# Half of w_down loaded early, and the last head's wo product summed in four column groups of one PSUM bank

## The chip, the cores and the metric

The kernel runs on one core of a Trainium2 chip. The metric is the device time of one execution in microseconds (us), the median of several runs. The profile measures the same execution from its first to its last instruction (the "span"); a run's time is about 1.8 us above its span (1285.2 against 1283.4 us for the profiled run of the kernel before).

Names used below: PE is TensorE, PEld its weight loads, DVE VectorE, ACT ScalarE, SP the engine that issues the DMAs. FFN2 is the product with w_down, PV the product with the values, oT its transposed and scaled result, FIN the product of oT with the last head's rows of wo. "Cold" means at the halved clock, "warm" at the full one.

## The reference, cut to what matters

One token is decoded. Attention has 8 key/value heads of 65536 positions and 16 query heads; a small FFN runs on the same normalized row, and everything is summed into one row of 448.

```python
# cut: shapes of the parts that matter
D = 448; Hq, Hkv, Sk, Dh = 16, 8, 65536, 256; F = 1792
xn = layernorm(x)                                # [1, 448]
o = softmax(q @ k.T * Dh**-0.5) @ v              # k, v caches: 2 x 268 MB in bf16
A = o.reshape(1, Hq * Dh) @ wo                   # wo [4096, 448]
g, u = silu(xn @ w_gate), xn @ w_up              # [1, 1792]
y = ((g * u) @ w_down) * sigmoid(xn @ w_r)       # w_down [1792, 448]
out = x + A + xn + y
```

The caches must be read once from HBM. All weights together are about 12 MB.

## The kernel before: the parts that the change touches

The caches go through a ring of four 4 MB slots. A "unit" is a quarter of a head; there are U = 4 units in each of 8 heads. While the keys of one head are worked on, the values of the head before it are. The last head's values are loaded alone, at the end, the very last slot in four pieces of 2, 1, 0.5 and 0.5 MB, so that little work is left when the last bytes land. The DMA program, issued in this order by SP:

```python
    item("wq", ...)
    for u in range(U):                       # keys of head 0
        ...
        if u == U // 2 - 1:
            item("wg", [... w_gate and w_up into w_area ...], [("QT",)])
            item("wd_a", [(wd_a[:, :], wd_src(0), "wd")])       # first half of w_down, 0.8 MB
    for t in range(NT): ...                  # keys of head h+1 and values of head h
    for t in range(NT, NU): ...              # values of the last head
    item("wd_b", [(w_area[:, 0:WDN], wd_src(1), "we0")], [("FFN1",)])   # second half, over w_gate
    for i in range(rep):                     # the last head's rows of wo, 2 x 0.23 MB
        item(("wo_end", i), [...])
    W("sp", "RESULT")
    ... out[0] <- res_bf[:, :]               # one row of 448
```

Between the last keys and the last values PE does the FFN as far as it can (`middle`); after the last values it does the rest (`ending`):

```python
    def middle():
        ...
        pe_ffn1(); pe_tot(NT); pe_ffn_hT()
        pe_ffn2(0, "wd_a", wd_a)             # 7 matmuls [128 x 1]^T @ [128 x 448]

    def ending():
        T = NU - 1
        dve_ob(T)                            # evict o from PSUM
        pe_oT(T)                             # transpose, and scale by 1/sum on DVE: oT
        pe_ffn2(1, "wd_b", w_area)           # 7 more
        ...
        O("dve", "BASE", ... base_f = ps_y * sigmoid + base_f ...)
        for i in range(rep):
            W_item("pe", ("wo_end", i))
            O("pe", ("FIN", i), lambda it, i=i: attn_mm(ps_fin, wo_end[:, :], [i], i == 0, i == rep - 1))  # 2 matmuls of 448
        O("dve", "RESULT", lambda it: nc.vector.tensor_tensor(out=res_bf[:, :], in0=ps_fin, in1=base_f, op=ALU.add))
```

PV, the product with the values, already uses four column groups of the PE array: four matmuls with four weight columns each run side by side and write to PSUM partitions 0, 32, 64 and 96.

## Time and profile before

| | before |
|---|---|
| time, median of 3 runs | 1284.51 us (1284.49 to 1285.25) |
| time and span of the profiled run | 1285.2 us, 1283.4 us |
| moved | 549 MB, 428 GB/s over the span |
| PE / DVE / ACT busy | 72% / 46% / 36% |
| from the start of the last PV to the end | 8.3 us |

First the page: the span in 40 slices, with the clock granted to PE in tenths (9 is full), the share of busy DMA engines and what they moved.

```profile
PEclk9988888998889988879888889888899887898876
DMA  9999999999999999999999999999999999999997
GB/s 405 427 433 427 433 432 431 430 431 432 432 433 431 433 430 433 430 433 430 433 432 432 432 431 432 429 433 433 431 432 432 432 430 433 431 431 433 431 429 318
```

DMA is full in every slice but the last, whatever PE's clock does. The view of waits, for the queue on SP that issues the DMAs, says what it waits for (us in total, times, longest):

```profile
SPq L776 <- PE ps_t L352: 855.3, 58, 20.9
SPq L776 <- PE ps_o L352: 182.8, 60, 18.6
SPq L776 <- PE ps_m L352: 145.9, 7, 22.7
```

These are waits for ring slots to come free, while the stream of earlier issues keeps the engines busy. So bytes set the time up to the last value, and what follows the last value is added to it. That tail, from the timeline (start, us, engine, line, operation, count, [idle before <- who ended it]):

```profile
1275.08 0.60 PE L352 MATMUL ps_o<-ring,p_sb 128*4 128x512 bf16 x4 [0.67 <-DMA ring<-in_A_v_cache_dram]
...
1276.79 0.16 DVE L561 TENSOR_TENSOR oT_sb<-ps_m,rs 128x4 bf16<-128x4 f32 x1 [0.36 <-PE ps_m L352]
...
1276.94 2.77 PE L352 MATMUL ps_t<-w_area,hT_sb 128*1 128x448 bf16 x7 [0.20 <-DMA w_area<-in_B_w_down_dram]
...
1279.51 1.70 PE L352 MATMUL ps_s<-wo_end,oT_sb 128*1 128x448 bf16 x4
...
1281.25 0.61 DVE L727 TENSOR_TENSOR res_bf<-ps_s,rowsf 1x448 bf16<-1x448 f32 x1 [0.82 <-PE ps_s L352]
1281.89 0.32 SPq L776 DMA_DIRECT2D out_dram<-res_bf  x1
```

The last PV begins at 1275.08 us, when its values have landed. oT is ready at 1276.95. The second half of w_down lands at about the same time: the wait of 0.20 us before the first matmul of `ps_t` is put down to it. Then come seven matmuls of w_down (`ps_t`) and four of wo (`ps_s`), 0.37 us from one to the next, then an add of 0.61 us over 448 columns in one partition, then the output. The windows view has the clock (columns: window and its us, then busy us and count of PE, PEld, DVE, ACT and POOL, the granted clock, DMA share, GB/s):

```profile
1274.00:1276.00 2.00, 1.01 (x8) 0.09 (x4) 0.27 (x1) 0.00 (x0) 0.00 (x0) 0.50 0.78 311
1276.00:1278.00 2.00, 1.32 (x7) 0.52 (x8) 0.59 (x2) 0.00 (x0) 0.00 (x0) 0.50 0.19 70
1278.00:1280.00 2.00, 2.00 (x7) 0.74 (x6) 0.24 (x1) 0.00 (x0) 0.00 (x0) 0.50 0.00 0
```

The clock in this stretch is half of the full one.

### The profile page before, as it was taken

Reading aid. Unit: us, or ns where it says so; the run is one execution under the profiler, and the core shown is the slowest. Engines: PE = TensorE matmul, PEld = TensorE weight load, DVE = VectorE, ACT = ScalarE, POOL = GpSimd, SP = SyncE. Lnnn points to the kernel's source line nnn. Section 1 sums busy time; section 2 is a strip of 40 time slices with the busy share of each in tenths; the row PEclk is TensorE's granted clock in tenths of the full one; section 3 lists DMA queues with packets and bytes.
Section 4 is the critical chain, followed back from the end, with each engine's and each line's share of the span. In section 5 each row is a group of like instructions: output and inputs, shape, how many; then the busy total and the mean of one; then the engine's idle time right before and its main releaser. Section 6 shows DMA issues by size and latency. Waiting matters only on the chain.

```text
span 1283.4 us, 22878 instructions
## 1 busy us (share of the span) xinstructions
PE 924.9 (72%) x9824; PEld 671.5 (52%) x9824; DVE 585.8 (46%) x1091; ACT 459.2 (36%) x655; POOL 4.5 (0%) x35
## 2 busy tenths in 40 slices
PE   3988766786666886666876667866668766678654
PEld 3867554465454565554654545654446544456411
DVE  4756443554344554444554445543445534455300
ACT  2645332353333443324433243432434333234300
POOL 1000000000000000000000000000000000000000
PEclk9988888998889988879888889888899887898876
DMA  9999999999999999999999999999999999999997
GB/s 405 427 433 427 433 432 431 430 431 432 432 433 431 433 430 433 430 433 430 433 432 432 432 431 432 429 433 433 431 432 432 432 430 433 431 431 433 431 429 318
DMA packets 22228, 549.22 MB, mean 428 GB/s; under 512 B 2371, under 2 KB 4422, under 8 KB 5190
## 3 DMA queue, kind: packets, MB, share of 16 engines
q1 hardware_dynamic: 22210, 549.04, 99.6%
q8 instruction: 8, 0.13, 0.0%
q14 instruction: 6, 0.05, 0.0%
q10 hardware_dynamic: 4, 0.00, 0.0%
HBM read 549.03 MB, written 0.00 MB: 428 GB/s over the span
## 4 chain that ended last, share of the span: by engine, by line
DMA 68%; PE 31%; SPq 0%; ACT 0%; issue 0%; DVE 0%
DMA ring<-in_A_k_cache_dram 63%; PE ps_t L352 24%; PE ps_q L352 5%; DMA w_area<-in_B_w_down_dram 3%; DMA ring<-in_A_v_cache_dram 2%; PE ps_s L352 1%; PE ps_m L352 1%; SPq L776 0%; ACT s L430 0%; DVE res_bf L727 0%; PE ps_o L352 0%
## 5 line engine op out<-in xcount | busy, mean ns | idle before, releaser
L352 PE MATMUL ps_t<-ident_f,ring 128*128 128x128 f32 x4096 | 568.8, 296 | 248.6 <-DMA ring<-in_A_k_cache_dram 229.5
L406 DVE COPY kt_buf<-ps_t 128x1024 bf16<-128x1024 bf16 x768 | 489.5, 683 | 420.9 <-PE ps_t L352 420.4
L352 PEld LDWEIGHTS ps_t<-ident_f,ring 128*128 128x128 f32 x4096 | 494.9, 152 | 354.2 <-DMA ring<-in_A_k_cache_dram 245.5
L408 ACT ACTIVATE kt_buf<-ps_t 128x1024 bf16<-128x1024 bf16 x256 | 261.9, 1023 | 356.1 <-PE ps_t L352 355.8
L430 ACT ACTIVATE s<-ps_q 98x512 bf16<-98x512 f32 x256 | 152.7, 597 | 288.1 <-PE ps_q L352 288.1
L352 PE MATMUL ps_o<-ring,p_sb 128*4 128x512 bf16 x2048 | 132.6, 401 | 67.0 <-DMA ring<-in_A_v_cache_dram 67.0
L352 PE MATMUL ps_q<-kt_buf,q_cur 128*2 128x512 bf16 x2048 | 166.2, 402 | 0.0
L352 PEld LDWEIGHTS ps_o<-ring,p_sb 128*4 128x4 bf16 x2048 | 47.7, 86 | 133.2 <-issue 75.5
L352 PEld LDWEIGHTS ps_s<-sel_bf,s 128*128 128x128 bf16 x1024 | 60.7, 99 | 54.1 <-ACT s L430 50.7
L540 DVE CAST ob_sb<-ps_o 100x512 bf16<-100x512 f32 x29 | 20.0, 691 | 142.8 <-PE ps_o L352 142.8
L352 PE MATMUL ps_s<-sel_bf,s 128*128 128x8 bf16 x1024 | 64.4, 169 | 22.6 <-ACT s L430 22.6
L497 ACT ACTIVATE p_sb<-S_sb 128x128 bf16<-128x128 bf16 x64 | 18.9, 307 | 136.2 <-PE ps_o L352 136.0
L576 DVE TENSOR_TENSOR rowsf<-ps_m,rowsf 1x448 f32<-1x448 f32 x28 | 17.1, 612 | 53.8 <-PE ps_m L352 53.8
L352 PEld LDWEIGHTS ps_q<-kt_buf,q_cur 128*2 128x2 bf16 x2048 | 27.1, 79 | 10.2 <-issue 5.0
L512 DVE RECIPROCAL rs<-ps_m 128x4 f32<-128x4 f32 x29 | 5.3, 182 | 52.8 <-PE ps_m L352 52.8
L352 PE MATMUL ps_m<-wo_cur,oT_sb 128*1 128x448 bf16 x112 | 25.7, 352 | 0.0
L352 PEld LDWEIGHTS ps_m<-rowsum,ones_f 128*128 128x128 f32 x116 | 15.1, 190 | 12.6 <-issue 12.6
L352 PE MATMUL ps_m<-rowsum,ones_f 128*128 128x2 f32 x116 | 17.6, 256 | 0.0
L352 PEld LDWEIGHTS ps_m<-wo_cur,oT_sb 128*1 128x1 bf16 x112 | 9.3, 83 | 13.5
L454 DVE CAST S_sb<-ps_s 128x256 bf16<-128x256 f32 x32 | 12.9, 404 | 4.3 <-PE ps_s L352 4.3
L487 ACT ACTIVATE S_sb<-S_sb,negmax 128x512 bf16<-128x512 bf16 x16 | 13.4, 864 | 3.6 <-DVE negmax L481 3.6
L456 DVE TENSOR_REDUCE m1p<-S_sb 128x2 f32<-128x256 bf16 x32 | 13.5, 421 | 1.1
(79 smaller groups left out, 138.3 us busy)
## 6 DMA issues: line engine op xcount, KB each, us to landing
ring<-in_A_k_cache_dram SPq DMA_DIRECT2D x64, 4096.0 KB, 25.0
ring<-in_A_v_cache_dram SPq DMA_DIRECT2D x62, 4096.0 KB, 32.0
ring<-in_A_v_cache_dram SPq DMA_DIRECT2D x2, 2048.0 KB, 28.1
w_area<-in_A_wq_dram SPq DMA_DIRECT2D x1, 3584.0 KB, 11.3
wo_cur<-in_A_wo_dram SPq DMA_DIRECT2D x7, 448.0 KB, 15.4
ring<-in_A_v_cache_dram SPq DMA_DIRECT2D x2, 1024.0 KB, 30.2
ring<-in_A_v_cache_dram SPq DMA_DIRECT2D x4, 512.0 KB, 31.4
w_area<-in_B_w_gate_dram SPq DMA_DIRECT2D x1, 1568.0 KB, 38.6
```

Source lines behind the costliest of these rows:

```text
L352: return pe.matmul(*a, **k)
L406: O(e, ("EV", s, m), lambda it: nc.vector.tensor_copy(out=kt[:, :], in_=tb[:, :]), f"ev{m}")
L408: O(e, ("EV", s, m), lambda it: nc.scalar.activation(out=kt[:, :], in_=tb[:, :], func=ACTF.Copy), f"ev{m}")
L430: O("act", ("EVQ", s), lambda it: nc.scalar.activation(out=s2[s % 2][0:QROWS, :], in_=ps_q[0:QROWS, :], func=ACTF.Copy), "evq")
L454: O("dve", ("SCOPY", u), lambda it: nc.vector.tensor_copy(out=S, in_=ps_sn))
L456: O("dve", ("SMAX", u), lambda it: nc.vector.tensor_reduce(out=m1p[:, :, k], in_=S.rearrange("p n i -> p i n"), axis=AX.X, op=ALU.max))
L487: O("act", ("EXP", h, i), lambda it, i=i: nc.scalar.activation(out=S_sb[:, :, i], in_=S_sb[:, :, i], func=ACTF.Exp, bias=negmax[:, i:i + 1 ...
L497: O("act", ("PC", t, c), lambda it: nc.scalar.activation(out=p_sb[:, c, :, :], in_=S_sb[:, n:n + CH, :], func=ACTF.Copy), "pc")
L512: O("dve", ("RS", t), lambda it: nc.vector.reciprocal(out=rs[:, :, :], in_=ps_m[0:P, C_TOT:C_TOT + NH * rep]))
L540: O("dve", ("OB", t), lambda it: nc.vector.tensor_copy(out=ob_sb[0:OROWS, :], in_=ps_o[0:OROWS, :]))
L576: O("dve", ("RES", t), lambda it: nc.vector.tensor_tensor(out=base_f, in0=ps_m[0:1, C_BIG:C_BIG + D], in1=base_f, op=ALU.add))
```

## The change

Intent: take everything but the last head's wo off the tail. Both halves of w_down are loaded with the gate weights near the start, and the FFN finishes before the last head's values. In the tail, the four wo matmuls of 448 columns become sixteen of 112 in four column groups of one PSUM bank, so that four run at a time. The base row (x + xn + FFN + the other heads) is put into the same PSUM groups beforehand by four one-row matmuls, so the last DVE operation is a copy of 112 columns on 97 partitions. The output then leaves from four partitions.

```diff
-            item("wd_a", [(wd_a[:, :], wd_src(0), "wd")])
+            item("wd", [(wd_a[:, :], wd_src(0), "wd"), (wo_end[:, :], wd_src(1)[:, 0:WON], "wd"),
+                        (w_area[:, WGN:WGN + WDN - WON], wd_src(1)[:, WON:WDN], "wd")])
 ...
-    item("wd_b", [(w_area[:, 0:WDN], wd_src(1), "we0")], [("FFN1",)])
     for i in range(rep):
-        item(("wo_end", i), [...])
+        item(("wo_end", i), [...], [("FFN2", 1)] if i == 0 else ())
-    ... out[0] <- res_bf[:, :]
+    ... out[0].rearrange("o (g n) -> (o g) n", g=NG) <- res_bf[0:P:P // NG, :]
 ...
     def middle():
-        pe_ffn2(0, "wd_a", wd_a)
+        for s in range(2):
+            pe_ffn2(s)
+        O("dve", "BASE", ...)                     # as before, but here
+        O("pe", "FIN_BASE", lambda it: [mm(fin(g), lhsT=ones_f[0:1, 0:1], rhs=base_f[0:1, g * DQ:(g + 1) * DQ],
+                                           start=True, stop=False, tile_position=(0, 32 * g)) for g in range(NG)][-1])
     def ending():
-        pe_ffn2(1, "wd_b", w_area)
-        O("dve", "BASE", ...)
         for i in range(rep):
-            O("pe", ("FIN", i), ... attn_mm(ps_fin, wo_end[:, :], [i], i == 0, i == rep - 1))
+            for hf in range(NH):
+                for g in range(NG):               # fin(g): one row of 112 at PSUM partition 32 * g
+                    mm(fin(g), lhsT=oT_sb[:, hf, i:i + 1], rhs=wo[:, i, hf, g * DQ:(g + 1) * DQ], start=False,
+                       stop=(i == rep - 1 and hf == NH - 1), tile_position=(0, 32 * g))
-        O("dve", "RESULT", ... tensor_tensor(out=res_bf[:, :], in0=ps_fin, in1=base_f, op=ALU.add))
+        O("dve", "RESULT", ... tensor_copy(out=res_bf[0:FROWS, :], in_=ps_s[0:FROWS, 0:DQ]))
```

(The diff is cut to its core; buffer shapes, semaphores and the arguments that do not matter are left out.)

More of the change, by code (lines that the diff above doesn't have):

```diff
@@ L69, in bass_parallel_sum__gqa_block_cached__moe_arch_mod__decode_kernel @@
     WQN, WGN, WDN, WON = RP * HqDh // 2, RP * F, FH * D, rep * NH * D
-    assert WQN >= max(WGN, WDN)
+    WD4 = WON // D
+    assert WQN >= WGN + (FH - WD4) * D and FH > WD4 and D % NG == 0
     sb = []
@@ L118, in bass_parallel_sum__gqa_block_cached__moe_arch_mod__decode_kernel @@
     xn_bf = S_("xn_bf", [1, D], BF16)
-    res_bf = S_("res_bf", [1, D], BF16)
+    res_bf = S_("res_bf", [P, D // NG], BF16)
     stat = S_("stat", [1, 16], FP32)
@@ L134, in bass_parallel_sum__gqa_block_cached__moe_arch_mod__decode_kernel @@
     ps_sn = ps_s[:, 0:SBN * rep].rearrange("p (n i) -> p n i", i=rep)
-    ps_fin = ps_s[0:1, 0:D]
+    DQ = D // NG
+    FROWS = 32 * (NG - 1) + 1
     ps_o = PS_("ps_o", [P, 2 * Dh], FP32)
@@ L149, in SEM @@
         return name
-    for n_ in ["pe", "act", "dve", "pool", "qk", "jt", "evq", "exp", "pc", "qc", "w0", "out", "wq", "wg", "wo", "wd", "we0", "we1", "we2"]:
+    for n_ in ["pe", "act", "dve", "pool", "qk", "jt", "evq", "exp", "pc", "qc", "w0", "out", "wq", "wg", "wo", "wd", "we0", "we1"]:
         SEM(n_)
@@ L241, in bass_parallel_sum__gqa_block_cached__moe_arch_mod__decode_kernel @@
             slot_item("v", t, c, last_parts(rounds[0]) if rounds[0] % NSLOT == NSLOT - 1 else None)
-    item("wd_b", [(w_area[:, 0:WDN], wd_src(1), "we0")], [("FFN1",)])
     for i in range(rep):
-        item(("wo_end", i), [(wo_view(wo_end[:, :])[:, i, :, :], wo_src(Hkv - 1)[:, i, :, :], "we%d" % (i + 1))])
+        item(("wo_end", i), [(wo_view(wo_end[:, :])[:, i, :, :], wo_src(Hkv - 1)[:, i, :, :], "we%d" % i)],
+             [("FFN2", 1)] if i == 0 else ())
     W("sp", "RESULT")
-    prog["sp"].append(("d", here[0], ("OUT",), (out[0], res_bf[:, :]), "out"))
+    prog["sp"].append(("d", here[0], ("OUT",), (out[0].rearrange("o (g n) -> (o g) n", g=NG), res_bf[0:P:P // NG, :]), "out"))
     items["out"] = ("out", 16)
@@ L626, in pe_ffn_hT, with pe_ffn2 @@
             out=hT_sb[:, :, :], in_=ps_m[0:P, C_HT:C_HT + FK].rearrange("p (t s) -> p t s", s=2)))
-    def pe_ffn2(s, key, area):
-        W_item("pe", key)
+    def pe_ffn2(s):
+        W_item("pe", "wd")
         W("pe", "HT")
@@ L633, in f @@
             for t in range(FH):
-                ins = mm(ps_y, lhsT=hT_sb[:, t, s:s + 1], rhs=area[:, t * D:(t + 1) * D],
+                area, o = (wd_a, t) if s == 0 else (wo_end, t) if t < WD4 else (w_area, WGN // D + t - WD4)
+                ins = mm(ps_y, lhsT=hT_sb[:, t, s:s + 1], rhs=area[:, o * D:(o + 1) * D],
                          start=(s == 0 and t == 0), stop=(s == 1 and t == FH - 1), skip_group_check=True)
@@ L690, in turn_B, with fin @@
         k_JT(s1 - 1)
+    def fin(g):
+        return ps_s[32 * g:32 * g + 1, 0:DQ]
     def middle():
@@ L701, in middle @@
         pe_ffn_hT()
-        pe_ffn2(0, "wd_a", wd_a)
+        for s in range(2):
+            pe_ffn2(s)
+        W("dve", "FFN2", 1)
+        W("dve", "SIG")
+        W("dve", "RES", NT - 1)
+        O("dve", "BASE", lambda it: nc.vector.scalar_tensor_tensor(out=base_f, in0=ps_y, scalar=stat[0:1, 6:7],
+                                                                  in1=base_f, op0=ALU.mult, op1=ALU.add))
+        W("pe", "BASE")
+        W("pe", "SCOPY", NU - 1)
+        O("pe", "FIN_BASE", lambda it: [mm(fin(g), lhsT=ones_f[0:1, 0:1], rhs=base_f[0:1, g * DQ:(g + 1) * DQ], start=True, stop=False,
+                                           tile_position=(0, 32 * g), skip_group_check=True) for g in range(NG)][-1])
     def turn_C(t):
@@ L713, in ending, with f @@
         pe_oT(T)
-        pe_ffn2(1, "wd_b", w_area)
-        W("dve", "FFN2", 1)
-        W("dve", "SIG")
-        W("dve", "RES", NT - 1)
-        O("dve", "BASE", lambda it: nc.vector.scalar_tensor_tensor(out=base_f, in0=ps_y, scalar=stat[0:1, 6:7],
-                                                                  in1=base_f, op0=ALU.mult, op1=ALU.add))
         W("pe", "OTSB", T)
-        W("pe", "SCOPY", NU - 1)
         for i in range(rep):
             W_item("pe", ("wo_end", i))
-            O("pe", ("FIN", i), lambda it, i=i: attn_mm(ps_fin, wo_end[:, :], [i], i == 0, i == rep - 1))
+            def f(it, i=i):
+                wo = wo_view(wo_end[:, :])
+                for hf in range(NH):
+                    for g in range(NG):
+                        ins = mm(fin(g), lhsT=oT_sb[:, hf, i:i + 1], rhs=wo[:, i, hf, g * DQ:(g + 1) * DQ], start=False,
+                                 stop=(i == rep - 1 and hf == NH - 1), tile_position=(0, 32 * g), skip_group_check=True)
+                return ins
+            O("pe", ("FIN", i), f)
         W("dve", "FIN", rep - 1)
-        W("dve", "BASE")
-        O("dve", "RESULT", lambda it: nc.vector.tensor_tensor(out=res_bf[:, :], in0=ps_fin, in1=base_f, op=ALU.add))
+        O("dve", "RESULT", lambda it: nc.vector.tensor_copy(out=res_bf[0:FROWS, :], in_=ps_s[0:FROWS, 0:DQ]))
     pool_setup()
```

## The prediction

> **What bounds it.** DMA. The page's DMA row reads 9 in 39 of 40 slices, at mostly 427 to 433 GB/s; 549 MB at 433 GB/s are 1268 of 1283.4 us. The DMA queue's waits are nearly all for freed ring slots, and a K load lands 25 us after issue, so two to three slots stay queued. Moving bytes inside the stream gains nothing; only what follows the last head's values counts.
>
> **The tail before** (timeline, end): the last V piece lands at 1275.08 us; PV, eviction, transpose and scaling give oT at 1276.95 (1.87 us). The second half of w_down lands at 1276.90. Its seven 448-column matmuls and four of wo run as one row at the halved clock (0.50 in the windows view), 0.37 us each, 1276.94 to 1281.21. The final add takes 0.61 us, to 1281.86; output issue and landing the last 1.54 us.
>
> **The change.**
> - w_down's second half (0.80 MB; 1.85 us at 433 GB/s) moves from behind the last V to the start. The stream stays full, so the last V lands 1.85 us later: 1276.93. This is the price.
> - Off the tail: seven matmuls, 2.6 us.
> - wo: 4 matmuls of 448 columns become 16 of 112 on four column groups. In PV, also on four groups, at the halved clock, four 512-column matmuls take 0.43 us together, their weight loads 0.14 us. A round of four should take 0.14 to 0.23 us, FIN 0.9 us with the drain, against 1.70. The Trainium skill ("TensorE: Matmul & The Clock Gate", "Measured speedup vs the span model") gives three column tiles 2.38x at 512 columns; at 112 I estimate under 2x, because weight loads dominate.
> - Final add: 448 columns on one row (612 ns) becomes a copy of 112. Casts of 512 and 256 columns took 691 and 404 ns, about 1.1 ns a column: 0.25 us.
> - Added in the middle, at about 1225 us: seven matmuls (2.6 us), the base operation (0.67 us), four fp32 one-row matmuls (under 1 us). The next PV starts about 4.3 us later, so freed slots issue later than 1228.7 relative to the stream. The stream has work until the piece landing at 1235.98, 7.3 us of slack; about 3 us remain.
>
> **Sum.** 1276.93 + 1.87 + 0.9 + 0.25 + semaphores 0.1 + 1.54 = 1281.6 us, against 1283.4: 1.8 us saved, of 3.65 us taken off the tail after oT; the other half is given back as later V data. Predicted 1282.7 us (0.14% faster), range 1281.8 to 1284.0. That is "same" at 2%; the whole tail after the last V is 0.65% of the span, so over 2% is out of reach.
>
> **What would show it.** Right: last V piece 1.85 us later; no DMA wait before FIN; FIN 0.9 us from first start to the copy's start; copy 0.25 us; DMA share unchanged at 1225 to 1245 us; tail from last V to end 6.5 us instead of 8.3. Wrong: the last V lands where it did (slack early in the stream; gain 3.6 us), or over 2 us later with a hole in DMA at 1236 to 1242 (PE's longer middle starved the ring).
>
> **What would make it wrong.** The slack eaten: that page (Part 1) says the clock halves after an idle window of about 3.4 us; this trace shows halved stretches of about 3.3 us after short gaps at 1213 and 1223. PE waiting for the base row could halve it again and slow PV (3.4 instead of 1.7 us a slot). Also: an output of four 224-byte rows landing slower than one of 896, up to 0.5 us; a full clock in the last 5 us; column-tiled one-column loads not overlapping (FIN 1.2 us or more); run scatter of 0.76 us.

## The result, and the profile after

The change ran in 1283.54 us (median of 4 runs, 1283.47 to 1283.79) against 1284.7 us for the kernel before on the same chip (4 runs, 1284.49 to 1285.25). The ratio is 0.9991 with an interval of 0.9973 to 1.0008. Ratios here are the mean time of one kernel's runs over that of the other's of the same rounds, so they are not quite the ratio of the medians. 1283.54 lies inside the predicted range. Later, on another job with 5 runs of the change and 9 of before, the medians were 1283.54 and 1285.12, a gain of 1.58 us. The output is correct.

The span fell from 1283.4 to 1281.6 us. The page after shows DMA still full:

```profile
PEclk9988878988789988889888899878898888998786
DMA  9999999999999999999999999999999999999998
GB/s 407 428 427 435 428 430 434 429 434 430 435 431 431 433 430 435 431 431 434 430 434 432 430 433 432 434 431 430 434 431 434 432 429 434 431 434 432 429 432 343
```

The tail after, from the timeline:

```profile
1277.05 0.39 PE L355 MATMUL ps_o<-ring,p_sb 128*4 128x512 bf16 x4 [0.84 <-DMA ring<-in_A_v_cache_dram]
...
1278.53 0.16 DVE L564 TENSOR_TENSOR oT_sb<-ps_m,rs 128x4 bf16<-128x4 f32 x1 [0.35 <-PE ps_m L355]
...
1278.74 0.45 PE L355 MATMUL ps_s<-wo_end,oT_sb 128*1 128x112 bf16 x16 [0.25 <-DVE oT_sb L564]
1279.24 0.27 DVE L745 CAST res_bf<-ps_s 97x112 bf16<-97x112 f32 x1 [0.56 <-PE ps_s L355]
1279.55 0.65 SPq L794 DMA_DIRECT2D out_dram<-res_bf  x1
```

And the windows of this trace, one microsecond each (columns as before):

```profile
1276.00:1277.00 1.00, 0.21 (x4) 0.00 (x0) 0.00 (x0) 0.00 (x0) 0.00 (x0) 1.00 0.26 100
1277.00:1278.00 1.00, 0.39 (x4) 0.09 (x4) 0.51 (x1) 0.00 (x0) 0.00 (x0) 1.00 0.04 16
1278.00:1279.00 1.00, 0.51 (x20) 0.36 (x20) 0.34 (x2) 0.00 (x0) 0.00 (x0) 0.94 0.00 0
```

The last PV starts 1.97 us later than before, since the 0.80 MB of w_down now come ahead of it. In the tail there is nothing between oT and the copy but 0.50 us of matmuls. Note the clock: 1.00 in this trace's tail, against 0.50 before. A second trace of the same kernel (run after_copy) had 0.50 all through the tail and the same span of 1281.6 us, but its last PV started 0.29 us earlier, so the equal spans are partly chance; its timeline:

```profile
1276.76 0.60 PE L355 MATMUL ps_o<-ring,p_sb 128*4 128x512 bf16 x4 [0.61 <-DMA ring<-in_A_v_cache_dram]
...
1278.67 0.54 PE L355 MATMUL ps_s<-wo_end,oT_sb 128*1 128x112 bf16 x16 [0.25 <-DVE oT_sb L564]
1279.26 0.27 DVE L745 CAST res_bf<-ps_s 97x112 bf16<-97x112 f32 x1 [0.65 <-PE ps_s L355]
1279.57 0.64 SPq L794 DMA_DIRECT2D out_dram<-res_bf  x1
```

| us | before | after | after, second trace | predicted |
|---|---|---|---|---|
| start of the last PV | 1275.08 | 1277.05 | 1276.76 | 1276.93 |
| from there to oT | 1.87 | 1.64 | 1.85 | 1.87 |
| oT to the start of the last DVE operation | 4.30 | 0.55 | 0.65 | 1.00 |
| last DVE operation | 0.61 | 0.27 | 0.27 | 0.25 |
| from its end to the end of the span | 1.54 | 2.09 | 2.07 | 1.54 |
| end of the span | 1283.4 | 1281.6 | 1281.6 | 1281.6 |
| granted clock at 1277 us | 0.50 | 1.00 | 0.50 | |

(All differences are taken from the starts and durations of the timeline. The predicted column splits the prediction's sum, with its 0.1 us for semaphores put into the third row.)

Two terms were mis-sized and, by luck, cancelled: the summing of wo was faster than predicted, the output slower.

### The profile page after: what moved, and what is told of

Same layout as the page of the kernel before. It is cut to its first block, busy times and chain, and to the rows that moved or that the text cites. A ratio compares the mean times of both kernels' runs of the same rounds, so it can differ in the third digit from the quotient of the medians.

```text
span 1281.6 us, 22918 instructions
## 1 busy us (share of the span) xinstructions
PE 921.9 (72%) x9844; PEld 670.7 (52%) x9844; DVE 585.7 (46%) x1091; ACT 459.4 (36%) x655; POOL 4.6 (0%) x35
## 4 chain that ended last, share of the span: by engine, by line
DMA 68%; PE 31%; SPq 0%; ACT 0%; issue 0%; DVE 0%
DMA ring<-in_A_k_cache_dram 63%; PE ps_t L355 24%; PE ps_q L355 5%; DMA ring<-in_A_v_cache_dram 5%; PE ps_s L355 1%; PE ps_m L355 1%; SPq L794 0%; ACT s L433 0%; PE ps_o L355 0%; DVE ob_sb L543 0%; DVE res_bf L745 0%; DVE oT_sb L564 0%
```

## The experiments

Twelve runs were made, two of them unchanged copies, each checked for its result (only out_row1 is wrong) and timed against the kernel before on the same chip. The kernel before had medians of 1285.12 to 1285.19 us in these four jobs; its executions, with before_copy's, lie between 1284.39 and 1285.65 us.

| run | median us | before, same job | difference | ratio, 95% interval |
|---|---|---|---|---|
| before_copy | 1285.23 | 1285.15 | +0.1 | 0.9998 (0.9984 to 1.0012) |
| move_only | 1284.41 | 1285.15 | -0.7 | 0.9994 (0.9981 to 1.0008) |
| cols_only | 1285.14 | 1285.15 | 0.0 | 1.0001 (0.9987 to 1.0015) |
| out_row1 (wrong) | 1283.02 | 1285.15 | -2.1 | 0.9983 (0.9970 to 0.9997) |
| after_copy | 1283.54 | 1285.12 | -1.6 | 0.9989 (0.9975 to 1.0002) |
| before_warm | 1283.74 | 1285.12 | -1.4 | 0.9990 (0.9976 to 1.0003) |
| after_warm | 1284.77 | 1285.12 | -0.4 | 0.9996 (0.9983 to 1.0010) |
| mid_10us | 1292.43 | 1285.12 | +7.3 | 1.0056 (1.0040 to 1.0071) |
| before_warm2 | 1283.60 | 1285.18 | -1.6 | 0.9988 (0.9975 to 1.0002) |
| after_warm2 | 1283.77 | 1285.18 | -1.4 | 0.9991 (0.9977 to 1.0004) |
| move_warm2 | 1283.97 | 1285.18 | -1.2 | 0.9992 (0.9978 to 1.0005) |
| late_tiles | 1282.99 | 1285.19 | -2.2 | 0.9983 (0.9969 to 0.9996) |

The stated intervals are about 0.14% wide each way (1.8 us), so most single ratios do not exclude 1 by themselves. The runs of one kernel lie much closer together: the five of the change between 1283.41 and 1283.83, the five of out_row1 between 1282.98 and 1283.04. Differences of 0.4 us and more are therefore read from the medians together with the term of the timeline that explains them, and differences of 0.2 us are not read at all.

### before_copy: the kernel before, unchanged

> The kernel before, unchanged, timed against itself for the noise floor, and a second trace of it. Ratio 1.000, interval under 0.1%. Theory C (the clock in the last 5 us is a matter of where the clock's window falls): the granted clock after the last V piece may differ from the 0.50 of the first trace, and then the tail from the last V to the end is up to 2 us shorter than 8.3 us. Rival: the tail is again 0.50 and 8.3 us.

No edit. The five runs lie between 1284.39 and 1285.49 us. The tail of this second trace was again at 0.50 from 1272 us on, with the last PV at 1275.34 and a span of 1283.7. So a cold tail is what two out of two traces of before show. Runs of before scatter over 1.3 us, those of the change over 0.4 us; whether the low ones of before had a faster clock in the tail is not shown, since no trace caught one.

### move_only: w_down early, the rest as before

> The w_down move alone: all of FFN2 and the base row before the last V, but wo as one row of four 448-column matmuls, the final add and a one-row output as before. Theory A (each part counts by itself in the tail): the last V lands 1.9 to 2.0 us later than before, seven matmuls (2.6 us cold, 1.3 us warm) leave the tail; span 0.7 us below before with a cold clock in both tails, and up to 0.6 us above before if before's tail is warm. Output landing as before, 1.5 us. Rival: nearly all of the 1.2 us gain comes from this part.

```diff
 # the change, with these parts put back
-        O("pe", "FIN_BASE", ...)                  # base row into PSUM
-        ... 16 matmuls of 112 in four groups ...
+        O("pe", ("FIN", i), ... attn_mm(ps_fin, wo_end[:, :], [i], i == 0, i == rep - 1))
-        O("dve", "RESULT", ... tensor_copy(...))
+        O("dve", "RESULT", ... tensor_tensor(out=res_bf[:, :], in0=ps_fin, in1=base_f, op=ALU.add))
```

It is 0.7 us faster than before, about half of the change's 1.6. The last PV started at 1277.35 us, so the price of the move was paid in full; the tail from there was 5.25 us to the span's 1282.6. The chain of waits (start, us, what) shows wo in one row, here with the clock falling from full to half inside it:

```profile
1279.04 1.39 PE ps_s L356 x4
...
1280.46 0.61 DVE res_bf L735
```

### cols_only: column groups, w_down's second half still last

> Column groups alone: w_down's second half still behind the last V; wo in four column groups, base row added last by four one-row matmuls, copy, four-row output. Theory A: last V lands as before (about 1275.1 us); the base row now ends the chain (FFN2, base 0.67, one-row matmuls 0.4, copy 0.27, output 2.05), span within 0.5 us of before: the column groups are worth nothing without the move. Rival: faster by 1 us or more, so the groups give the gain by themselves.

```diff
 # the kernel before, with the four-group sum, the copy and the four-row output; the base row is added last
+            ... 16 matmuls of 112, start=(i == 0 and hf == 0) ...
+        W("pe", "BASE")
+        O("pe", "FIN_BASE", lambda it: [mm(fin(g), lhsT=ones_f[0:1, 0:1], rhs=base_f[...], start=False, stop=True, ...) ...])
```

No gain at all (1285.14 against 1285.15). The chain is what was expected: FFN2, the base operation, the one-row matmuls, then the copy:

```profile
1276.97 1.71 PE ps_t L353 x5
...
1279.78 0.68 DVE rowsf L722
...
1280.51 0.43 PE ps_s L353 x8
...
1280.97 0.27 DVE res_bf L742
```

The sum in groups waits behind FFN2 on one side and the base row on the other. Its copy still ended 0.6 us earlier than before's final add (1281.24 against 1281.86 us), and the four-row output, 0.5 us longer (see out_row1), gave most of that back; column groups with a one-row output were not run. The two parts of the change are not additive: -0.7 and 0.0 alone, -1.6 together, because the groups only shorten the chain once FFN2 and the base row are out of it.

### out_row1: the output from one partition

> The change as it is, except that the output is written as one row of 448 from partition 0 (wrong on purpose: only its first 112 columns are results, the rest zeros). Theory B: the four-row output costs 0.5 us (in the trace after, 2.09 us from the copy's end to the span's end against 1.54 us before; issue 0.65 against 0.32): here issue 0.32 us, about 1.55 us to the end, and the run 0.5 us faster than the change. Rival: the 2.09 us come from something else (a late instruction fetch, say) and stay.

```diff
-    ... out[0].rearrange("o (g n) -> (o g) n", g=NG) <- res_bf[0:P:P // NG, :]
+    ... out[0] <- res_bf[0:1, :]                # wrong on purpose: 112 results, then zeros
```

1283.02 against the change's 1283.54 (the two jobs' medians of before agree within 0.03 us). In its timeline:

```profile
1279.42 0.27 DVE L747 CAST res_bf<-ps_s 97x112 bf16<-97x112 f32 x1 [0.65 <-PE ps_s L356]
1279.72 0.32 SPq L796 DMA_DIRECT2D out_dram<-res_bf  x1
```

From the copy's end (1279.69) to the span's end (1281.2) it takes 1.5 us, as before, against 2.07 to 2.09 in the change; the issue alone takes 0.32 instead of 0.64. So the four-row output costs 0.5 us. This is a third of what the change gained, given back in its last instruction.

### after_copy, before_warm, after_warm: the clock in the tail

> The change, unchanged, on the same chip as the next three. The first job had the before at 1284.7 us (4 runs), the second at 1285.15 (9 runs). Theory S (the gain is the 1.8 us of the two profiled spans, and the first median of before was low because its runs lie between 1284.5 and 1285.3): 1.6 to 1.8 us faster than before here, 1283.5 us. Rival: 1.2 us faster again, and the profiled before was an unlucky one.

> The kernel before, with idle-filling 512-column matmuls into an unused PSUM bank between the value loads of the last two units, so that the clock should be full in the tail (the last unit's loop on the PE is unrolled for that). Theory C: of the cold tail, eleven 448-column matmuls at 0.37 us would take 0.19: 2.0 us off, PV 0.2 us more; if the granted clock is 1.0 from 1272 us to the end, 2.0 to 2.3 us faster than before, and as fast as the change. If the timed runs of before are partly at full clock already, less. Rival: below 0.5 us, because the tail waits for landing data and not for the PE.

> The same filling in the change. Its tail holds only 0.5 us of matmuls after oT, measured at full clock as 0.48 us and at the halved clock (run with one output row) as 0.57 us, and the PV 0.39 against 0.63 us: at most 0.4 us faster than the change, on average 0.2 us. If before_warm gains 2 us and this 0.2 us, then most of what the change gained could be had by the clock alone.

```diff
 # in PV of the last two units (unrolled on PE), after each piece of values
+            n_ = {64: 24 if (t, c) != (NU - 1, 0) else 12, 32: 6, 16: 3, 8: 4 if k < len(got) - 1 else 0}[J] ...
+            O("pe", ("WARM", t, c, k), lambda it, n_=n_: [mm(ps_q[:, 0:512], lhsT=ident_bf[:, :], rhs=wd_a[:, 0:512],
+                                                             start=True, stop=True) for _ in range(n_)][-1])
```

after_copy settles the gain of the change: 1.58 us, close to the 1.8 us between the two profiled spans. The first job's 1.16 us had two of before's four runs near the low end of its range.

before_warm gained 1.4 us, less than the expected 2.0 to 2.3, because the filling was too heavy: it ran past the landing of the values, and the last PV began at 1276.53 us where the values land at about 1275.1 in other traces. In after_warm the same delay, to 1278.52 us, made the run 1.2 us slower than the change, where 0.2 us faster was expected. That is a fault of the experiment and says nothing about the change, except that its tail is as exposed to a late PE as before's.

### before_warm2, after_warm2, move_warm2: a lighter filling

> The kernel before with a lighter filling. In before_warm the filling ran on past the landing of the last values: the last PV began at 1276.53 us, although they land at about 1275.1. Theory C: last PV at 1275.1 to 1275.4 us at full clock, oT at 1276.7, FFN2 and wo at full clock (1.4 and 0.8 us), span near 1281.3 us: 2.0 us faster than before, and no slower than the change without any of its parts. Rival: the clock falls again with the lighter filling, and the gain is under 1 us.

> The change with the lighter filling. Theory C: 0.2 to 0.4 us faster than the change, span near 1281.4 us, within 0.3 us of before_warm2: with the clock full, the change is worth nothing, since the 1.3 us of matmuls it takes off the tail cost it 1.85 us of data. Rival: the gains add, and it is 1 us or more faster than before_warm2.

> The w_down move alone (wo, the final add and the output in one row as before), with the lighter filling. Theory C: slower than before_warm2 by 0.3 to 0.6 us (1.85 us of data for 1.4 us of matmuls), span near 1281.7 us. Rival: as fast as or faster than before_warm2.

```diff
-            n_ = {64: 24 if (t, c) != (NU - 1, 0) else 12, 32: 6, 16: 3, 8: 4 if k < len(got) - 1 else 0}[J] ...
+            n_ = {(NU - 2, 0): [24], (NU - 2, 1): [34], (NU - 1, 0): [11], (NU - 1, 1): [4, 2, 3, 0]}...[k]
```

Now the last PV starts at 1275.47 us in before_warm2, 0.1 to 0.4 us later than in the traces of the unfilled kernel, and the profile puts its wait down to the landing of the values again. The tail of before_warm2, the kernel before with nothing but filling, from the timeline:

```profile
1275.47 0.39 PE L352 MATMUL ps_o<-ring,p_sb 128*4 128x512 bf16 x4
...
1276.96 0.16 DVE L565 TENSOR_TENSOR oT_sb<-ps_m,rs 128x4 bf16<-128x4 f32 x1 [0.35 <-PE ps_m L352]
...
1277.35 1.49 PE L352 MATMUL ps_t<-w_area,hT_sb 128*1 128x448 bf16 x7 [0.43 <-DMA w_area<-in_B_w_down_dram]
...
1278.67 0.92 PE L352 MATMUL ps_s<-wo_end,oT_sb 128*1 128x448 bf16 x4
1278.87 0.67 DVE L722 SCALAR_TENSOR_TENSOR rowsf<-ps_t,stat,rowsf 1x448 f32<-1x448 f32 x1 [1.75 <-PE ps_t L352]
1279.65 0.61 DVE L731 TENSOR_TENSOR res_bf<-ps_s,rowsf 1x448 bf16<-1x448 f32 x1
```

And the windows view of the same run:

```profile
1276.00:1278.00 2.00, 0.91 (x8) 0.51 (x9) 0.77 (x2) 0.00 (x0) 0.00 (x0) 1.00 0.26 102
1278.00:1280.00 2.00, 1.59 (x9) 0.51 (x6) 1.03 (x2) 0.00 (x0) 0.00 (x0) 1.00 0.00 0
```

The eleven matmuls take 0.19 us each instead of 0.37, and the kernel before becomes as fast as the change: 1283.60 us against 1283.54, a gain of 1.6 us where 2.0 were expected. It still waits 0.2 us for w_down, which landed at 1277.35. Of the three fully clocked kernels, before_warm2 (1283.60), after_warm2 (1283.77) and move_warm2 (1283.97), none is ahead by the stated intervals. But all five executions of move_warm2 (1283.81 to 1284.30) lie above all five of before_warm2 (1283.34 to 1283.79), 0.4 us at the medians, as it should be if 1.85 us of data are paid for 1.4 us of matmuls; those of after_warm2 overlap both. The filling did not make the change faster. The expected 0.2 to 0.4 us did not appear: in its trace the last PV started at 1277.29 us, 0.2 to 0.5 us later than in the two traces of the change, again waiting for its values. Whether the filling delays the landing or this is scatter (move_only, unfilled, had 1277.35) stays open.

### mid_10us: how much slack the stream has in the middle

> The change, with 47 matmuls of 512 columns (10 us at full clock, up to 20 at half) between the base row and the values of the last head. Theory M (slack in the middle): in the change the first slot is freed at 1232.5 us and the stream has work until 1238.0, so 10 us more lets the DMA run dry for about 10 - 5.6 + 2 = 6.5 us: 6 to 7 us slower than the change, and the last V lands that much later. Rival: no slower, because more is queued than the trace shows.

```diff
     middle()
+    O("pe", "MORE", lambda it: [mm(ps_q[:, 0:512], lhsT=ident_bf[:, :], rhs=wd_a[:, 0:512], start=True, stop=True) for _ in range(47)][-1])
```

It is 8.9 us slower than the change, more than the 6 to 7 us expected. The windows view of this run shows the stream dry (the last two columns are DMA share and GB/s):

```profile
1235.00:1236.00 1.00, 1.00 (x7) 0.41 (x6) 0.00 (x0) 0.00 (x0) 0.00 (x0) 1.00 0.57 233
1236.00:1237.00 1.00, 1.00 (x6) 0.48 (x5) 0.00 (x0) 0.00 (x0) 0.00 (x0) 1.00 0.14 57
...
1238.00:1239.00 1.00, 1.00 (x6) 0.42 (x5) 0.00 (x0) 0.00 (x0) 0.00 (x0) 1.00 0.00 0
...
1243.00:1244.00 1.00, 1.00 (x24) 0.46 (x20) 0.00 (x0) 0.31 (x1) 0.00 (x0) 1.00 0.00 0
```

The first slot was issued at 1243.42 us, 10.95 us later than in the change (1232.47), and the last PV started at 1286.53, 9.5 us later. So the change has some 1.5 us of slack left there, not 5.6; this is the trace of the slowest of the four executions, and with the medians' 8.9 us, if the first slot was as late there, it would be 2. My slack was counted from the issue to the landing of the last queued piece; but most of the DMA engines ran dry before that (57% of them busy in 1235 to 1236 us, 14% in the next). And after the issue at 1243.42 us no data moved before 1244 us. That these two account for the whole difference is argued, not shown by a run of its own.

### late_tiles: a version built on this

> A version built on what the runs showed, meant to beat both kernels. Data that lands behind the last V costs nothing up to about 2 us behind it, because oT is ready only 1.6 to 1.9 us after the last V. So of w_down's second half three tiles go early and four (0.46 MB, 1.06 us) stay behind the last V; the sigmoid is folded into hT, and all of FFN2 is added straight into the four column groups, with no base operation on the vector engine after it. Theory D (each byte early costs its 1/433 us per KB at the end): last V at 1276.0 us, 1.0 to 1.1 us earlier than in the change; wo lands at about 1278.1, FIN ends at 1278.5, the copy starts 0.6 to 0.7 us earlier than the change's 1279.25, time 1282.9 us. Rival: the late tiles and wo land later than that and hold FIN back, and it is as slow as the change, 1283.5 us.

```diff
 # against the change
-            item("wd", [(wd_a, ...), (wo_end, 4 tiles), (w_area[:, WGN:...], 3 tiles)])
+            item("wd", [(wd_a, ...), (w_area[:, WGN:WGN + EARLY * D], wd_src(1)[:, 0:EARLY * D], "wd")])      # EARLY = 3
+    item("wd_late", [(w_area[:, 0:LATE * D], wd_src(1)[:, EARLY * D:WDN], "wl")], [("FFN1",)])               # LATE = 4, behind the last V
     ...
+        O("pe", "SIGB", lambda it: mm(ps_m[0:P, C_BC:C_BC + 1], lhsT=ones_f[0:1, 0:P], rhs=stat[0:1, 6:7], ...))   # sigmoid to all partitions
-        O("dve", "HT", ... tensor_copy(out=hT_sb, ...))
+        O("dve", "HT", ... tensor_scalar(out=hT_sb, ..., scalar1=sig_b[:, 0:1], op0=ALU.mult))
-        FFN2 into ps_y; O("dve", "BASE", ...); O("pe", "FIN_BASE", ...)
+        O("pe", "FIN_BASE", ...)                              # then every FFN2 tile as 4 matmuls of 112 into fin(g)
     def ending():
         pe_oT(T)
+        pe_ffn2("wd_late", 1, [(1, EARLY + t, w_area, t * D) for t in range(LATE)])
```

It ran in 1282.99 us, within 0.1 of what was expected, and is correct: 2.2 us faster than before and about 0.6 us faster than the change. Its tail, from the timeline:

```profile
1276.06 0.60 PE L356 MATMUL ps_o<-ring,p_sb 128*4 128x512 bf16 x4 [0.64 <-DMA ring<-in_A_v_cache_dram]
...
1277.65 0.54 PE L356 MATMUL ps_s<-w_area,hT_sb 128*1 128x112 bf16 x16
1277.76 0.16 DVE L565 TENSOR_TENSOR oT_sb<-ps_m,rs 128x4 bf16<-128x4 f32 x1 [0.36 <-PE ps_m L356]
...
1277.98 0.60 PE L356 MATMUL ps_s<-wo_end,oT_sb 128*1 128x112 bf16 x16
1278.64 0.28 DVE L746 CAST res_bf<-ps_s 97x112 bf16<-97x112 f32 x1 [0.72 <-PE ps_s L356]
```

The last PV starts at 1276.06 us, 0.7 to 1.0 us earlier than in the change, because 0.46 MB of w_down stay behind the values; they have landed when oT's transpose is done, and their sixteen matmuls of 112 fit beside the scaling of oT on DVE. All this happens at the halved clock.

## Why the prediction was right, and where it was not

**DMA bounds the kernel, and only the tail counts.** Right. DMA stays full, and the last PV moved by 1.97 us in the first pair of traces. The mean over three traces with w_down's second half behind the values (before 1275.08, before_copy 1275.34, cols_only 1275.11) is 1275.18, over four of the change's order (after 1277.05, after_copy 1276.76, out_row1 1276.90, move_only 1277.35) it is 1277.02: 1.84 us, where the prediction had 1.85 from 0.80 MB at 433 GB/s. Single traces scatter by up to 0.6 us.

**The time.** Predicted 1282.7, measured 1283.54, in the range. The predicted span of 1281.6 us was met exactly, by the cancelling errors below, but the time was taken by subtracting 1.8 us from a median of 1284.51, while the profiled run behind the span was one of 1285.2. The median of three lay at the low end of a kernel whose runs spread from 1284.39 to 1285.65. The gain came out as 1.16 us in the first job and 1.58 in the second.

**The summing of wo.** Predicted 0.9 us because "weight loads dominate"; measured 0.50 at the full clock and 0.59 at half. The step that failed is the size of a round of four. The loads do not dominate; they overlap. In late_tiles, 28 one-column matmuls of 112 columns in four groups start between 1225.92 and 1226.26 us at a granted clock of 1.00, 12 ns apart on average, and each has its own weight load of 79 to 84 ns. Against four matmuls of 448 the groups gave 1.74 to 0.59 us at the halved clock (before against after_copy, from the first start to the start of the last DVE operation), a factor of 2.9, and 0.96 to 0.50 at the full clock (move_warm2 against after), 1.9. The Trainium skill ("TensorE: Matmul & The Clock Gate", "Measured speedup vs the span model") has 2.38x for three column tiles; the "under 2x" that I made of it was wrong at the halved clock, for which it was made.

**The copy.** Predicted 0.25, measured 0.27 us.

**The output.** Predicted unchanged at 1.54 us, with up to 0.5 us named as a risk; measured 2.07 to 2.09, and out_row1 shows that the four-row output is the cause (the four partitions and the shorter rows were changed together). The errors cancel, which is luck: by the table 0.35 to 0.45 us won at wo and 0.1 to 0.2 up to oT, 0.55 lost at the output.

**The tail "6.5 us instead of 8.3".** This was a slip: 6.5 is 8.3 less the net gain, while the prediction's own sum gives 1281.6 - 1276.9 = 4.7 us. Measured: 4.55 and 4.85 us.

**The middle.** The stream did not run dry, as predicted, but the slack was mis-sized: 1.5 to 2 us were left, not 3, and mid_10us shows what happens beyond it. PE's clock was full during PV there in the trace after, which helped: the first freed slot was issued only 1.8 us later relative to the stream (1232.47 - 1228.69 - 1.97), not 4.3. At the halved clock a unit's PV took 3.58 us (before, at 1245.79) where the first slot was freed after 1.94 here, so most of the slack would have been gone; this is an estimate.

**What the prediction did not see.** It read the halved clock in the tail and costed with it, but did not ask what the same tail costs at the full clock. The Trainium skill ("TensorE: Matmul & The Clock Gate", "What's actually happening") describes two clock states, chosen by activity in a free-running window of 3.4 us. The granted clock in the tail was 0.50 or 1.00, PV's bursts of up to 3.6 us in every 9.7 kept it up only at times, filled gaps did from 1255 us on. The clock records of the traces show more. In all 14 traces every stretch of one granted clock, first and last aside, is a whole multiple of 3.413 us. Of the 1247 windows of that length at 0.50, PE was busy in 462 for a share of 0.80 or more, and the next window was at 1.00 each time; in 777 for less than 0.79, and the next was never at 1.00; of the eight in between, seven were followed by 1.00. So the place where a window happens to cut PV's bursts decides the clock of the tail. These are the windows before the tail of after, busy for 0.81 and followed by 1.00, and of after_copy, 0.78 and followed by 0.50:

```profile
1272.06:1275.47 3.41, 2.77 (x24) 0.51 (x24) 0.00 (x0) 0.00 (x0) 0.00 (x0) 0.50 0.95 380
...
1272.38:1275.80 3.42, 2.66 (x28) 0.36 (x20) 0.00 (x0) 0.00 (x0) 0.00 (x0) 0.50 0.90 358
```

At the full clock the moved matmuls are worth 1.3 us, less than the 1.85 us their data cost at the front. With filling, the kernel before equals the change. So the gain is real, but it is a gain over a cold PE: the change makes the tail nearly independent of the clock (0.50 against 0.59 us of matmuls after oT), and that is its use.

## What to carry to other kernels

In a kernel bound by its DMA stream, moving bytes from behind the last needed byte to the front costs their full transfer time at the end; leave behind it whatever lands before its consumer is ready, and move only the rest. Cost a short tail at both clocks, since a PE that waits for data can be cold, and spread narrow last-row work over column groups, counting what a many-row output costs to send. Count a queue's slack to where its engines run dry (at 1235 to 1237 us in mid_10us), not to where the last transfer lands.

## What the Trainium skill lacked or had wrong

- "TensorE: Matmul & The Clock Gate", "The mechanism": one line of the list there says that weight loads overlap matmuls in flight only when the row group differs. Taken alone it does not fit: here all matmuls use all 128 rows and differ only in the column group, and 28 of them with a load each start 12 ns apart, while a load is recorded with 79 to 84 ns. The loads overlapped. The paragraph above that line also allows it for a background weight buffer; which of the two ways it was is not in these traces.
- Same page, "Back-to-back issue gap": an issue floor of about 25 ns for a matmul is stated, without saying whether it holds across column groups. Part 3 of the page has closer starts for tiles packed together, but gives no rate for a stream of them. 12 ns from one start to the next were recorded with four column groups of 112 columns (late_tiles, granted clock 1.00).
- Same page, Part 1: it does not say how busy PE must be in a window for the clock to rise. In these runs the limit lies between 0.79 and 0.80 of a 3.41 us window (1247 windows, see above). For falling no such sharp limit shows: windows at 1.00 with PE busy for up to 0.62 were followed by 0.50, others with as little as 0.41 by 1.00; so no wholly idle window was needed.
- "DMA: Bandwidth & Descriptors": no cost by the number of rows is given for a small output. One row of 896 bytes took 0.32 us to issue and 1.5 us to the end of the span, four rows of 224 bytes on four partitions 0.64 and 2.1.
- Same page: no figure is given for how far apart the engines of one queue finish. Here one hardware queue's packets fill 99.6% of the engines' span (before), and at the end of the stream the share of busy engines falls over more than two microseconds (after_copy: 0.95, 0.66, 0.23 and 0.02 in the four from 1274 to 1278 us). Which engines are late is not in these traces.
